# Softmax attention with PSUM banks picked by age instead of by name, and with new orders for its pairs of units

## Chip, cores and metric

One core of one Trainium2 chip runs the whole program. The metric is device time in microseconds (us), the median of several runs. A profile of one execution gives each engine's instructions: PE (TensorE matmuls), PEld (its weight loads), DVE (VectorE), ACT (ScalarE), POOL (GpSimd) and SP (SyncE, which issues DMAs).

## What is computed

A transformer block of 2048 tokens, 512 channels, in fp32: attention with 32 heads of 16 channels behind a layer norm, then a gated MLP whose gate mixes tokens. The change lies in the attention.

```python
def _A_ref(x, wqkv, wo):
    B, S, D = x.shape
    H = 32; Dh = D // H
    ...
    scale = Dh ** -0.5
    scores = jnp.einsum("bhqd,bhkd->bhqk", q, k) * scale
    p = _softmax(scores, axis=-1)
    o = jnp.einsum("bhqk,bhkd->bhqd", p, v)
    ...
h = x + _A_ref(_layernorm(x, axis=-1), A_wqkv, A_wo)
h2 = h + _B_ref(_layernorm(h, axis=-1), B_w_in, B_w_sp, B_b_sp, B_w_out)
```

## The kernel before

The program has three stages: projections (to about 165 us), the attention (to about 1350 us), and the rest. In the attention, heads go in eight groups of four (`hg`), queries in four blocks of 512 (`qb`), keys in sixteen blocks of 128 (`kb`). A **unit** is one `(hg, qb, kb)`: four score products of 128 keys by 512 queries, one for each head, four exponentials on ACT into one `pt` tile, and four products of `pt` with the values, which add up in one PSUM bank, `pv` (`weigh`, L718). A **block** is the sixteen units of one `(hg, qb)`; at its end ACT copies `pv` out (`gather`, L736).

The softmax needs the maximum of each row first. So eight more products for two units compute scores for a later block (`max_pair`, L218): four of kind M and two of kind m, each reduced by DVE (L241), and v and u, where ACT takes an absolute value (L246) and DVE combines it (L250). M uses the array's rows from 64 on, m, v and u those from 0 on. Of the score products, Sa uses the rows from 0 on and Sb those from 64 on. Two products that stand next to each other on different rows run side by side.

Every product, S or M, m, v, u, takes one of **seven PSUM banks**: m0 to m2 are numbers 0 to 2 (`ps_m`), s0 to s3 are numbers 3 to 6 (`ps_s`). The eighth is `pv`. A bank is free again when ACT or DVE has read it; PE waits for that at the product's weight load.

The order of the work is written out in lists that `play` (L751) goes through, for PE, ACT and DVE alike. In `"Sa5 M6 m3"` the letter is the kind of product and the number is the bank. `h` weighs half of the oldest finished unit (256 queries), `V` the whole of it. `N` reduces finished maxima on DVE, `T` transposes them and sends them off by DMA (or inverts sums), `G` is `gather`. `ORDER` (L42) is played for a pair of units (16 products), `FIRST_TWO` (L46) for a block's first two pairs (32 products), `START` (L45) once, for the very first pair. A list is cut into **groups** of products by its weighings: in `ORDER` six products, h, four, h, six, V. There are 245 such pairs: START 1, FIRST_TWO 30 times two, ORDER 184. The last eleven pairs are scheduled by other code, which the change leaves alone.

An ACT or DVE instruction that needs two semaphores gets an extra instruction ahead of it, which waits for the one (here PE's), while the instruction itself waits for the other. The first exponential of a unit is such a case, since its `pt` tile is new.

Of the kernel before, what the change touches and what calls it, by code (L numbers as in the profile page):

```python
# [34 lines left out]
MB = 3  # L35
# [3 lines left out]

ORDER = "Sa5 M6 m3 M2 v4 Sb1 h Sb6 u0 M5 Sa4 h Sb2 m3 Sb6 Sa1 N M4 Sa0 V T".split()  # L42

FOUR = "S S S S V S S S S H H H H S S S S V S S S S V V".split()
START = "Sa5 M6 m3 M2 v4 Sb1 f Sb6 u0 M5 Sa4 Sb2 m3 Sb6 Sa1 M4 Sa0 V".split()  # L45
FIRST_TWO = ("M5 Sa3 M2 Sa4 Sb1 Sb0 m6 h Sa4 M2 v3 m5 Sb1 M6 h u2 G Sa5 Sb3 m0 Sb4 M1 Sa6 V "  # L46
             "v0 M2 Sa3 M5 u1 Sb4 h h Sa2 Sb5 m6 M3 Sb1 Sa0 V").split()
RG = 64
VW = DH + 1
NF = 5  # L50
# [9 lines left out]
def block_kernel(ctx: ExitStack, tc: tile.TileContext, x, wqkv, wo, w_in, w_sp4, b_sp, w_out, out):  # L60
# [152 lines left out]
    def bank(i):  # L213
        if i in more:
            return more[i]()
        return ps_m.tile([P, 512], F32, name=f"m{i}")
# [59 lines left out]
    def max_rows():  # L276

        g, parts = turned.pop(0)
        t = sm.tile([P, 32], F32, name="mturned")
        nc.vector.transpose(t, parts.bitcast(F32).rearrange("p t j i -> p (t j i)"))  # L280
        for n in range(P // 32):
            for j in range(2):
                r0 = RG * j + KS
                nc.sync.dma_start(
                    qst[g][r0:r0 + 2].bitcast(F32).rearrange("r p (c n s) -> r (p c) n s", n=4, s=32)[:, :, n],
                    t[32 * n + 16 * j:32 * n + 16 * j + 16, :])


    with ExitStack() as pre:
# [178 lines left out]
        todo, done = [], [0]  # L468
# [203 lines left out]
    def invert():  # L672

        hg, cols, sums, pool = sums_.pop(0)
        rc = pool.tile([P, 16], F32, name="rcp")
        nc.vector.reciprocal(rc, sums)
        for j in range(4):
            nc.sync.dma_start(r_scr[head(hg, j % 2, j // 2), cols].rearrange("(p c) -> p c", c=16),
                              rc[32 * j:32 * j + 32, :])
# [3 lines left out]
    with ExitStack() as at:  # L683
# [10 lines left out]
        def new_pt():  # L694
            return pp.tile([P, 4, 512], F32, name="pt")

        def product(out, hg, qb, kb, t, p):

            r = slice(RG * t, RG * t + KM)
            nc.tensor.matmul(out, kst[hg % 2][r, p, kb * P:(kb + 1) * P], qst[hg * NQ + qb][r, p, :],  # L700
                             start=True, stop=True)

        def exp(out, scores):
            nc.scalar.activation(out, scores, AF.Exp, scale=DH ** -0.5)  # L704
# [13 lines left out]
        def weigh(unit, pt, places, cols=slice(0, 512)):  # L718

            hg, qb, kb = unit  # L720
            if kb == 0 and cols.start == 0:
                pv[0] = ps_v.tile([P, 512], F32, name="pv")
            for t, p in sorted(places, key=places.get):
                j = 2 * t + p
                c = (4 * kb + j) * VW
                nc.tensor.matmul(pv[0][32 * j:32 * j + 32, cols], vst[hg % 2][:, c:c + 32],  # L726
                                 pt[:, places[t, p], cols], start=kb == 0,
                                 stop=kb == NB - 1 and cols.stop == 512)
# [3 lines left out]
        def gather(hg, qb, pool=sm):  # L732

            o = pp.tile([P, 512], F32, name="o", bufs=1)
            if pool is sm and not later:
                nc.scalar.activation(o, pv[0], AF.Copy)  # L736
            else:
                nc.vector.tensor_copy(o[:, :256], pv[0][:, :256])
                if later and pool is sm:
                    nc.vector.tensor_copy(o[:, 256:], pv[0][:, 256:])  # L740
                else:
                    nc.scalar.activation(o[:, 256:], pv[0][:, 256:], AF.Copy)
            cols = slice(qb * 512, (qb + 1) * 512)
            sums = pool.tile([P, 16], F32, name="sums")
            for j in range(4):
                h = head(hg, j % 2, j // 2)
                nc.sync.dma_start(o_scr[h * DH:(h + 1) * DH, cols], o[32 * j:32 * j + DH, :])
                nc.sync.dma_start(sums[32 * j:32 * j + 32, :], o[32 * j + DH:32 * j + VW, :])
            sums_[0] = (hg, cols, sums, pool)

        def play(order, units):  # L751

            ending = pending[:]
            pending[:] = ends
            ends.clear()
            units = list(units)
            open_ = []
            for x in order:  # L760
                if x[0] == "S":
                    if not open_:
                        open_.extend([units.pop(0), new_pt(), {}])
                    unit, pt, places = open_
                    t = "ab".index(x[1])
                    p = sum(u == t for u, _ in places)
                    out = bank(int(x[2:]))
                    product(out, *unit, t, p)
                    exp(pt[:, len(places), :], out)
                    places[t, p] = len(places)  # L770
                    if len(places) == 4:
                        waiting.append([tuple(open_), 0])
                        open_.clear()
                elif x == "h":
                    h = waiting[0][1]
                    weigh(*waiting[0][0], slice(256 * h, 256 * h + 256))
                    waiting[0][1] += 1
                    if h:
                        done[0] = waiting.pop(0)[0][0]
                elif x == "V":  # L780
                    done[0] = waiting[0][0][0]
                    weigh(*waiting.pop(0)[0])
                elif x == "G":
                    gather(*done[0][:2])
                elif x == "f":

                    pv[0] = ps_v.tile([P, 512], F32, name="pv")
                    for j in range(4):
                        nc.tensor.matmul(pv[0][32 * j:32 * j + 32, :], vst[0][:, :32],
                                         vst[0][:, :512], start=True, stop=True)  # L790
                elif x == "N":
                    if ending:
                        ending.pop()()
                elif x == "T":
                    if turned:
                        max_rows()
                    elif done[0] is not None and done[0][2] == 5 and sums_:
                        invert()
                else:
                    steps_of[x[0]].pop(0)(int(x[1:]))  # L800
            assert not ending and not open_ and not units

        waiting, done, doubles = [], [None], []

        def play_four(units):

# [24 lines left out]
        steps_of = {kind: [] for kind in "Mmvu"}  # L831
# [43 lines left out]
        with tc.manual_schedule(engines={E.PE, E.Activation, E.DVE, E.SP}):  # L875
            for n in range(0, len(units), 2):
# [9 lines left out]
                steps, place = n // 2 + LEAD < 8 * HG * NQ, n % NB // 2  # L886
# [10 lines left out]
                if steps:  # L897
                    if place or not n:
                        if place != 1 or n == 2:
                            play(ORDER if n else START, units[n:n + 2])  # L900
                    else:
                        play(FIRST_TWO, units[n:n + 4])
                elif n % 4 == 0:
                    if n == 504:
                        load_o(h_rows[3])
                    play_four(units[n:n + 4])
                elif n < 492:
                    if pending:
                        pending.pop()()
                    for i in range(2):  # L910
                        pt = new_pt()
                        for p in range(2):
                            for step in score(units[n + i], p, pt):
                                step()
                        if i:
                            more_h(4)
                        weigh(*waiting.pop(0)[0])
                        waiting.append([(units[n + i], pt, PLACES), 0])
                    if turned:
                        max_rows()  # L920
# [17 lines left out]
    def quarter(pool, name, tag):  # L938
        return pool.tile([P, HB, PITCH], F32R, name=name, tag=tag)[:, :, :FC]

    T = {n: [quarter(zc, n, f"{n}_{i}") for i in range(2)]
         for n in ("t3", "t2", "n4", "t1")}
# [175 lines left out]
    with ExitStack() as fin:  # L1118
# [36 lines left out]
        f = [Slot(fs, f"f{i}") for i in range(3)]  # L1155
# [148 lines left out]
        def fetch_h(p):  # L1304
            h = [f2.tile([P, D], F32, name=f"h{i}", bufs=2 - i) for i in range(2)]
            for i in (1, 0):
                nc.sync.dma_start(h[i], h_scr[rows(p, i), :])
            return h
# [46 lines left out]
        for p in range(HB):  # L1355
            (q, _, z1), last = nxt, p + 1 == HB
            nxt = None if last else fetch(p + 1)
            h = fetch_h(p)
# [96 lines left out]
```

## Time and profile before

| what | value |
|---|---|
| three runs | 1821.95, 1823.29, 1823.30 us, median 1823.29 |
| the profiled execution | 1821.23 us, span 1819.4 us |
| PE, DVE, ACT busy over the span | 1811.2, 1505.7, 1380.1 us |
| PE, DVE, ACT busy in 600 to 700 us | 100.0, 93.0, 96.9 us |
| granted TensorE clock | 1.00 |

A row of the timeline has start, duration, engine, line, operation, output<-input and a count; what stands in brackets is the idle time ahead of it and what ended it. In the timeline tiles are named without their numbers: `s<-kst,qst` of L236 is a product for the maxima in one of the banks s0 to s3, `m<-qst,kst` of L700 is a score product in one of m0 to m2.

### The profile page before, as it was taken

What the parts mean: (1) busy time and instruction counts of PE and PEld (TensorE: products, weight loads), DVE (VectorE), ACT (ScalarE), POOL (GpSimd) and SP (SyncE); (2) the same over time, 40 slices, a digit from 0 to 9 for tenths busy, and PEclk for the clock granted to TensorE, in tenths of its full rate; (3) what the DMA queues carried; (4) which work ended last, traced back from release to release, by engine and by line L of the source; (5) the groups of instructions that cost most, each with busy time, mean ns of one, the idle gap of its engine ahead of it and who ended that gap; (6) DMA issues with size and microseconds to landing.
All of it is one profiled execution on the core that took longest, in us unless ns stands there. A gap on an engine that the chain in (4) does not pass through costs nothing.

```text
span 1819.4 us, 36269 instructions
## 1 busy us (share of the span) xinstructions
PE 1811.2 (100%) x13362; PEld 1040.9 (57%) x13362; DVE 1505.7 (83%) x3030; ACT 1380.1 (76%) x2676; POOL 226.0 (12%) x305
## 2 busy tenths in 40 slices
PE   9999999999999999999999999999999999999999
PEld 6875444444444444444444444444438889999998
DVE  6587999999999999999999999999926677877664
ACT  3224999999999999999999999999994444434221
POOL 2241000011010100000000000000110755001111
PEclk9999999999999999999999999999999999999999
DMA  6788111221120211022012011100215554768562
GB/s 197 196 194 204 42 25 31 48 56 29 40 58 17 55 41 25 20 48 39 14 40 43 19 38 40 26 14 17 40 51 138 168 171 162 229 193 279 188 197 90
DMA packets 148761, 160.17 MB, mean 88 GB/s; under 512 B 63096, under 2 KB 93320, under 8 KB 147240
## 3 DMA queue, kind: packets, MB, share of 16 engines
q1 hardware_dynamic: 143800, 146.44, 30.3%
q10 hardware_dynamic: 4752, 11.41, 1.6%
q8 instruction: 105, 1.72, 0.4%
q14 instruction: 72, 0.59, 0.1%
q0 software_dynamic: 32, 0.01, 0.0%
HBM read 101.26 MB, written 55.61 MB: 86 GB/s over the span
## 4 chain that ended last, share of the span: by engine, by line
PE 99%; DVE 1%; ACT 0%; issue 0%; DMA 0%; SPq 0%; DVEq 0%; ACTq 0%
PE pv L726 30%; PE s L700 15%; PE m L700 9%; PE s L236 8%; PE acc L107 6%; PE acc L109 6%; PE acc L108 5%; PE m L236 4%; PE g L109 4%; PE g L108 4%; PE g L107 4%; PE acc L645 2%; PE tp L1323 1%; PE acc L1344 0%; PE tp L1019 0%; PE tp L390 0%
## 5 line engine op out<-in xcount | busy, mean ns | idle before, releaser
L241 DVE TENSOR_REDUCE mx<-s 128x1 f32<-128x512 f32 x1135 | 727.7, 684 | 79.4 <-PE s L236 53.7
L704 ACT ACTIVATE pt<-s 128x512 f32<-128x512 f32 (+1 forms) x1084 | 650.6, 666 | 3.1 <-PE s L700 1.6
L726 PE MATMUL pv<-pt,vst 128*32 128x256 f32 (+1 forms) x6048 | 590.9, 466 | 0.0
L704 ACT ACTIVATE pt<-m 128x512 f32<-128x512 f32 x920 | 536.8, 618 | 37.6 <-PE s L236 26.2
L236 PE MATMUL s<-kst,qst 48*128 48x512 f32 x1135 | 445.2, 433 | 0.0
L700 PE MATMUL s<-qst,kst 50*128 50x512 f32 x1128 | 432.6, 456 | 0.5 <-ACT pt L704 0.5
L700 PEld LDWEIGHTS s<-qst,kst 50*128 50x128 f32 x1128 | 190.2, 184 | 266.6 <-DVE mx L241 179.7
L700 PE MATMUL m<-qst,kst 50*128 50x512 f32 x920 | 320.0, 432 | 0.0
L241 DVE TENSOR_REDUCE mx<-m 128x1 f32<-128x512 f32 x373 | 250.9, 684 | 11.5 <-PE m L236 10.9
L726 PEld LDWEIGHTS pv<-pt,vst 128*32 128x32 f32 x6048 | 123.6, 108 | 213.5 <-issue 202.0
L236 PEld LDWEIGHTS s<-kst,qst 48*128 48x128 f32 x1135 | 189.8, 185 | 58.8 <-ACT pt L704 27.5
L700 PEld LDWEIGHTS m<-qst,kst 50*128 50x128 f32 x920 | 150.7, 184 | 105.8 <-DVE mx L241 87.3
L250 DVE CUSTOM_DVE_ANT_0 ab<-m,ab 128x512 f32<-128x512 f32 x249 | 169.6, 681 | 0.6 <-PE m L236 0.5
L236 PE MATMUL m<-kst,qst 48*128 48x512 f32 x373 | 144.2, 416 | 0.0
L236 PE MATMUL m<-uvs,qst 48*128 48x512 f32 x282 | 137.1, 486 | 0.0
L246 ACT ACTIVATE ab<-s 128x512 f32<-128x512 f32 x215 | 136.8, 636 | 0.0
L101 POOL CAST mparts<-nm 128x16 fp32r<-128x16 f32 x32 | 6.3, 196 | 883.0 <-DVE nm L254 883.0
L236 PE MATMUL s<-uvs,qst 48*128 48x512 f32 x215 | 84.2, 392 | 0.0
L959 ACT ACTIVATE ws<-a 128x512 fp32r<-128x512 f32 x80 | 45.8, 621 | 48.7 <-PE g L109 23.8
L1038 ACT ACTIVATE z<-acc 128x464 f32<-128x464 f32 (+2 forms) x64 | 27.6, 457 | 67.3 <-PE acc L109 67.3
L236 PEld LDWEIGHTS m<-uvs,qst 48*128 48x128 f32 x282 | 51.6, 183 | 39.8 <-DVE mx L241 37.5
L107 PE MATMUL acc<-wi,hT 128*128 128x464 f32 (+2 forms) x196 | 72.8, 371 | 0.0
(210 smaller groups left out, 2592.7 us busy)
## 6 DMA issues: line engine op xcount, KB each, us to landing
a<-in_w_sp SPq DMA_DIRECT2D x80, 256.0 KB
qst<-q_scr SPq DMA_DIRECT2D x192, 64.0 KB
z_scr<-z ACTq DMA_DIRECT2D x32, 344.0 KB
kst<-k_scr SPq DMA_DIRECT2D x42, 256.0 KB
k_scr<-part SPq DMA_DIRECT2D x16, 512.0 KB
q_scr<-part SPq DMA_DIRECT2D x16, 512.0 KB
z<-z_scr SPq DMA_DIRECT2D x14, 344.0 KB
b<-z_scr SPq DMA_DIRECT2D x24, 172.0 KB
```

What stands on the lines that cost most here:

```text
L107: nc.tensor.matmul(ps, lh, rh, start=first, stop=False)
L108: nc.tensor.matmul(ps, lh, rl, start=False, stop=False)
L109: nc.tensor.matmul(ps, ll, rh, start=False, stop=last)
L236: nc.tensor.matmul(acc, q[r, p, c], keys[r, p], start=True, stop=True)
L241: nc.vector.reduce_max(at(t, e if t else e - 1), acc, axis=AX.X)
L246: nc.scalar.activation(ab[0], acc, AF.Abs)
L250: nc.vector.tensor_tensor_reduce(ab[0], acc, ab[0], 0.5, LOW, ALU.add, ALU.max, at(0, 0))
L645: yield nc.tensor.matmul(acc, o2[b][:, d, :], wo2[a][:, d, :], start=i == 0, stop=i == 3 * DB - 1)
L700: nc.tensor.matmul(out, kst[hg % 2][r, p, kb * P:(kb + 1) * P], qst[hg * NQ + qb][r, p, :], start=True, stop=True)
L704: nc.scalar.activation(out, scores, AF.Exp, scale=DH ** -0.5)
L726: nc.tensor.matmul(pv[0][32 * j:32 * j + 32, cols], vst[hg % 2][:, c:c + 32], pt[:, places[t, p], cols], start=kb == 0, stop=kb == NB - 1 ...
L959: nc.scalar.activation(hi, src, AF.Copy)
```

## The change

The number behind a letter is no longer a bank but a place in a list of the seven banks by age. `by_age` takes the bank at that place out of the list (0 is the one whose last use began longest ago), and puts it at the end. All three orders are new. `N` and `T` stand earlier in `ORDER`. The number of products of each kind, of weighings and of units is the same in each list. `ORDER` still has groups of six, four and six. `FIRST_TWO` had groups of seven, six, seven, six and six products, with two halves side by side in `h h`; it now has six, four, six, six, four and six.

```diff
-ORDER = "Sa5 M6 m3 M2 v4 Sb1 h Sb6 u0 M5 Sa4 h Sb2 m3 Sb6 Sa1 N M4 Sa0 V T".split()
+ORDER = "Sa0 M0 Sa2 M0 m1 Sb0 h Sb0 Sa0 M0 N m0 h v0 Sb1 Sa0 M0 u1 T Sb0 V".split()
...
-FIRST_TWO = ("M5 Sa3 M2 Sa4 Sb1 Sb0 m6 h Sa4 M2 v3 m5 Sb1 M6 h u2 G Sa5 Sb3 m0 Sb4 M1 Sa6 V "
-             "v0 M2 Sa3 M5 u1 Sb4 h h Sa2 Sb5 m6 M3 Sb1 Sa0 V").split()
+FIRST_TWO = ("Sb0 m0 M2 Sa0 M1 Sa0 h v0 Sb0 M0 u1 h G Sa0 M1 Sb0 Sa0 m1 Sb0 V Sb0 m0 Sa0 M0 Sa1 "
+             "M0 h Sb0 Sa1 M0 m0 h v0 M0 Sa0 Sb0 u1 Sb0 V").split()
...
+        def by_age(place):
+
+            ages.append(ages.pop(int(place)))
+            return ages[-1]
...
-                    out = bank(int(x[2:]))
+                    out = bank(by_age(x[2:]))
...
-                    steps_of[x[0]].pop(0)(int(x[1:]))
+                    steps_of[x[0]].pop(0)(by_age(x[1:]))
...
-        waiting, done, doubles = [], [None], []
+        waiting, done, doubles, ages = [], [None], [], list(range(MB + 4))
```

ACT in the middle of the attention, from the first product of a pair's third group on. Tiles are named with their numbers: `m2_14028` is bank m2, the number behind counts tiles. Before, the first row waits for PE and for a second semaphore, and the absolute value (`ab`) comes sixth:

```order
L704 ACTIVATE pt_14027<-m2_14028 128x512 [waits PE_49,Activation_49]
L704 ACTIVATE pt_14027<-s3_14034 128x512 [waits PE_49]
L704 ACTIVATE pt_14027<-m1_14037 128x512 [waits PE_49]
L704 ACTIVATE pt_14027<-m0_14043 128x512 [waits PE_49]
L704 ACTIVATE pt_14050<-s2_14051 128x512 [waits PE_49,Activation_49]
L246 ACTIVATE ab_14065<-s1_14063 128x512 [waits PE_49]
L704 ACTIVATE pt_14050<-m1_14067 128x512 [waits PE_49]
```

The same place of ACT in the changed program (its lines are one lower):

```order
L245 ACTIVATE ab_14029<-s3_14027 128x512 [waits PE_49]
L703 ACTIVATE pt_14013<-s0_14031 128x512 [waits PE_49]
L703 ACTIVATE pt_14013<-m2_14034 128x512 [waits PE_49]
L703 ACTIVATE pt_14013<-s1_14043 128x512 [waits PE_49]
L703 ACTIVATE pt_14050<-m1_14051 128x512 [waits PE_49,Activation_49]
L703 ACTIVATE pt_14050<-s2_14057 128x512 [waits PE_49]
L703 ACTIVATE pt_14050<-m2_14066 128x512 [waits PE_49]
```

The absolute value has moved from the sixth place to the first, and what comes first now waits for PE alone.

PE, the second group of the next pair, up to the first product of its third group, before. The last of the four products, in bank s1, waits for ACT:

```order
L700 MATMUL s3_14074<-qst_12329,kst1_1733 128x512 [waits DVE_49]
L236 MATMUL m0_14077<-uvs1_1734,qst_12877 128x512
L236 MATMUL s2_14080<-kst1_1733,qst_12877 128x512 [waits Activation_49]
L700 MATMUL s1_14083<-qst_12329,kst1_1733 128x512 [waits Activation_49]
L726 MATMUL pv_13925<-pt_14027,vst1_104 32x256 x4
L700 MATMUL m2_14091<-qst_12329,kst1_1733 128x512 [waits DVE_49]
```

The same place of PE in the changed program:

```order
L699 MATMUL s1_14073<-qst_12329,kst1_1733 128x512
L699 MATMUL m1_14077<-qst_12329,kst1_1733 128x512 [waits Activation_49]
L235 MATMUL s3_14080<-kst1_1733,qst_12877 128x512 [waits DVE_49]
L235 MATMUL s2_14083<-kst1_1733,qst_12877 128x512 [waits Activation_49]
L725 MATMUL pv_13912<-pt_14013,vst1_104 32x256 x4
L235 MATMUL s0_14090<-uvs1_1734,qst_12877 128x512 [waits DVE_49]
```

The last product of this group was Sa in s1, and is m in s2; it waits in both for the sixth row of ACT above (s1_14063 before, s2_14057 now). The first product of the third group was Sb and is v.

PE in `FIRST_TWO`, around its fourth weighing, before: both halves stand side by side (x8 is two times four products).

```order
L236 MATMUL s2_2380<-kst0_105,qst_1334 128x512
L236 MATMUL m1_2383<-uvs0_106,qst_1334 128x512 [waits DVE_49]
L700 MATMUL s1_2386<-qst_1185,kst0_105 128x512 [waits Activation_49]
L726 MATMUL pv_2365<-pt_2308,vst0_103 32x256 x8
L700 MATMUL m2_2398<-qst_1185,kst0_105 128x512 [waits DVE_49]
```

The same place of PE in the changed program:

```order
L699 MATMUL m0_10082<-qst_8483,kst1_1733 128x512 [waits DVE_49]
L235 MATMUL s3_10085<-kst0_105,qst_9035 128x512 [waits Activation_49]
L725 MATMUL pv_10064<-pt_10045,vst1_104 32x256 x3
L725 MATMUL pv_10064<-pt_10045,vst1_104 32x256 [waits Activation_49]
L699 MATMUL s2_10092<-qst_8483,kst1_1733 128x512
L699 MATMUL s0_10096<-qst_8483,kst1_1733 128x512 [waits DVE_49]
L235 MATMUL m2_10099<-kst0_105,qst_9035 128x512 [waits Activation_49]
L235 MATMUL m1_10102<-kst0_105,qst_9035 128x512 [waits Activation_49]
L725 MATMUL pv_10064<-pt_10045,vst1_104 32x256 x4
```

The halves are now apart, with a group of four products between them, so PE changes from products to weighing six times in a block's first two pairs where it did so five times.

More of the change, by code (lines that the diff above doesn't have):

```diff
@@ L37 @@
 FIRST = 1
-ORDER = "Sa5 M6 m3 M2 v4 Sb1 h Sb6 u0 M5 Sa4 h Sb2 m3 Sb6 Sa1 N M4 Sa0 V T".split()
+ORDER = "Sa0 M0 Sa2 M0 m1 Sb0 h Sb0 Sa0 M0 N m0 h v0 Sb1 Sa0 M0 u1 T Sb0 V".split()
 FOUR = "S S S S V S S S S H H H H S S S S V S S S S V V".split()
-START = "Sa5 M6 m3 M2 v4 Sb1 f Sb6 u0 M5 Sa4 Sb2 m3 Sb6 Sa1 M4 Sa0 V".split()
-FIRST_TWO = ("M5 Sa3 M2 Sa4 Sb1 Sb0 m6 h Sa4 M2 v3 m5 Sb1 M6 h u2 G Sa5 Sb3 m0 Sb4 M1 Sa6 V "
-             "v0 M2 Sa3 M5 u1 Sb4 h h Sa2 Sb5 m6 M3 Sb1 Sa0 V").split()
+START = "Sa0 M0 Sa2 M0 m1 Sb0 f Sb0 Sa0 M0 m0 v0 Sb1 Sa0 M0 u1 Sb0 V".split()
+FIRST_TWO = ("Sb0 m0 M2 Sa0 M1 Sa0 h v0 Sb0 M0 u1 h G Sa0 M1 Sb0 Sa0 m1 Sb0 V Sb0 m0 Sa0 M0 Sa1 "
+             "M0 h Sb0 Sa1 M0 m0 h v0 M0 Sa0 Sb0 u1 Sb0 V").split()
 RG = 64
```

## The prediction, on record before the run

> **What bounds the kernel now.** I read the page first: which engine is busy, and what the chain that ended last is made of.
>
> ```profile
> PE 1811.2 (100%) x13362; PEld 1040.9 (57%) x13362; DVE 1505.7 (83%) x3030; ACT 1380.1 (76%) x2676; POOL 226.0 (12%) x305
> ...
> PE 99%; DVE 1%; ACT 0%; issue 0%; DMA 0%; SPq 0%; DVEq 0%; ACTq 0%
> ```
>
> PE looks like the only bound, and DMA and SP's queue release nothing. But the change works in the attention alone, so next I took busy time by stretch, and the copies that end its blocks.
>
> ```profile
> 600.00:700.00 100.00, 100.00 (x848) 42.28 (x844) 93.00 (x180) 96.86 (x195) 2.88 (x11) 1.00 0.19 38
> ```
>
> ```profile
> L736 ACT ACTIVATE o<-pv x30: 675/692/701, 207.4 to 1302.9; 128x512 f32<-128x512 f32 x30
> ```
>
> PE, ACT and DVE (the first, fourth and third share) are all nearly full, and 29 blocks of eight pairs take 1302.9 - 207.4 = 1095.5 us, 37.78 each. With three engines this close, a share decides nothing; I follow one ordinary pair, from the timeline.
>
> ```profile
> 603.33 0.49 PE L700 MATMUL m<-qst,kst 50*128 50x512 f32 x1
> ...
> 603.33 0.50 PE L236 MATMUL s<-kst,qst 48*128 48x512 f32 x1
> ...
> 603.91 0.60 ACT L704 ACTIVATE pt<-m 128x512 f32<-128x512 f32 x1 [0.17 <-PE s L236]
> ...
> 604.23 1.07 PE L726 MATMUL pv<-pt,vst 128*32 128x512 f32 x8
> 604.41 0.59 ACT L704 ACTIVATE pt<-s 128x512 f32<-128x512 f32 x1
> 604.89 1.09 ACT L704 ACTIVATE pt<-m 128x512 f32<-128x512 f32 x2
> ...
> 605.23 0.50 PE L700 MATMUL s<-qst,kst 50*128 50x512 f32 x1
> ...
> 605.58 0.40 PE L236 MATMUL m<-kst,qst 48*128 48x512 f32 x1
> ...
> 605.79 1.29 DVE L241 TENSOR_REDUCE mx<-s 128x1 f32<-128x512 f32 x2 [0.39 <-PE s L236]
> ...
> 605.81 0.39 PE L700 MATMUL m<-qst,kst 50*128 50x512 f32 x1
> 605.84 0.63 ACT L704 ACTIVATE pt<-s 128x512 f32<-128x512 f32 x1
> ...
> 606.13 0.64 PE L726 MATMUL pv<-pt,vst 128*32 128x256 f32 x8
> 606.32 0.64 ACT L246 ACTIVATE ab<-s 128x512 f32<-128x512 f32 x1
> 606.70 0.50 PE L700 MATMUL s<-qst,kst 50*128 50x512 f32 x1
> ...
> 607.01 0.18 PEld L700 LDWEIGHTS s<-qst,kst 50*128 50x128 f32 x1
> ...
> 607.04 0.47 PE L700 MATMUL s<-qst,kst 50*128 50x512 f32 x1
> ...
> 607.44 0.64 PE L726 MATMUL pv<-pt,vst 128*32 128x256 f32 x8
> ...
> 608.01 0.49 PE L700 MATMUL m<-qst,kst 50*128 50x512 f32 x1
> ```
>
> ACT is idle once in the pair: at 603.91 it waits for the third group's first product, although PE began that at 603.33. PE waits once too: the weight load at 607.01 (Sa4, the second group's last) comes just after the `ab` that ends at 606.32 + 0.64 = 606.96 and frees its bank; its product takes 0.47 where the one beside it on time took 0.39. The two waits make one **loop**:
>
> - third group starts 603.33, its first product ends 0.49 later, ACT starts 0.09 after that;
> - that exponential takes 0.60, to 604.51; five more ACT instructions end at 606.96, 2.45 us later, 0.49 each;
> - 0.05 to the weight load, 0.43 from there to the weighing at 607.44, 0.57 to the next third group at 608.01.
>
> The sum is 0.49 + 0.09 + 0.60 + 2.45 + 0.05 + 0.43 + 0.57 = 4.68, and 608.01 - 603.33 is 4.68. So an ordinary pair takes what this loop takes. PE without the stall: groups of six take 606.13 - 605.23 = 0.90 (a slot of two products 0.23, from 605.58 to 605.81), one of four 0.67, a half 0.57, the whole 1.00; in all 2 x 0.90 + 0.67 + 2 x 0.57 + 1.00 = 4.61. ACT's nine instructions need 9 x 0.49 = 4.41. DVE is idle 0.39 ahead of 605.79. A new order can therefore win at most 0.07 in an ordinary pair, and can lose much more.
>
> **The ordinary pair after.** The number of products, weighings and groups is the same, so PE's 4.61 and ACT's 4.41 stay. What can change is the loop. I followed the new list's places to banks (the rows of ACT and PE in the section on the change): the second group's last product, m, gets the bank of Sa2 from the group before. ACT's order from the third group is v, Sb, Sa, Sb, Sa, Sa2: Sa2 is the sixth instruction, as `ab` was. **The loop has the same links and the same five steps of 0.49.** One link differs. Its first ACT instruction was the first exponential of a unit, which waits for PE through an extra instruction; now it is v's absolute value, which waits for PE itself. Two rows of the projections, of equal shape, show what that is worth:
>
> ```profile
> 161.62 0.39 PE L109 MATMUL acc<-xT,wqk 128*128 128x512 f32 x1
> ...
> 162.05 0.60 ACT L99 ACTIVATE part<-acc 128x512 fp32r<-128x512 f32 x1 [2.95 <-PE acc L109]
> ...
> 164.36 0.39 PE L109 MATMUL acc<-xT,wqk 128*128 128x512 f32 x1
> ...
> 164.84 0.60 ACT L99 ACTIVATE part<-acc 128x512 fp32r<-128x512 f32 x1 [2.19 <-PE acc L109]
> ```
>
> The one at 162.05 holds the wait for PE itself and starts 0.04 after the product's end. At 164.84 the wait stands in the extra instruction, and it is 0.09, as at 603.91. No row of the attention shows ACT idle ahead of a direct wait; the nearest there is DVE's at 605.79, 0.06 after the product that began at 605.23 ended. So the link saves 0.03 to 0.05; I take 0.05, as ACT's own rows have it, which gives 4.63, still above PE's 4.61. Mid-way the extra instruction costs nothing: 605.84 has one ahead of it, and its end, 606.47, is 0.49 after the one before it.
>
> 184 pairs play `ORDER`; 30 of them follow `FIRST_TWO` and are counted with it. 154 x 0.05 = **7.7 us**.
>
> **A block's first two pairs.** Here the trace has
>
> ```profile
> 619.29 0.50 PE L236 MATMUL s<-kst,qst 48*128 48x512 f32 x1
> ...
> 626.01 1.07 PE L726 MATMUL pv<-pt,vst 128*32 128x256 f32 x16
> ...
> 627.01 0.50 PE L700 MATMUL m<-qst,kst 50*128 50x512 f32 x1
> ...
> 627.60 0.60 ACT L704 ACTIVATE pt<-m 128x512 f32<-128x512 f32 x1 [0.21 <-PE s L700]
> ...
> 629.05 0.49 PE L700 MATMUL s<-qst,kst 50*128 50x512 f32 x1
> ...
> 633.64 0.50 PE L700 MATMUL s<-qst,kst 50*128 50x512 f32 x1
> ```
>
> 9.76 for the two pairs and 4.59 for the ordinary one behind, 14.35 in all. ACT's 16 exponentials, two absolute values and the copy need 19 x 0.49 = 9.31; 0.45 is lost, part of it at 627.60. In the old list same-row products stand together (Sb1 Sb0; v3 m5), so its 32 products need 18 slots of two where 16 would do. The new list always alternates: 16 slots. Against that it changes to weighing six times, not five. One change costs 0.90 - 3 x 0.23 = 0.21 in a group and 0.57 - 0.43 = 0.14 at a half (side by side two halves take 1.00, so 0.43 more than one), together 0.35; two slots save 0.46. PE gains 0.1.
>
> Going through the list with these durations, ACT still has 0.2 us of work when the second group's first product is ready, 0.3 to 0.4 at the third to fifth, and runs dry only at the sixth, whose first product is v again. There it loses what an ordinary pair loses: 4.63 - 4.41 = 0.22. That gives 9.31 + 0.22 = 9.53, and 4.63 behind it: 14.16, a gain of 0.19; 30 x 0.19 = **5.7 us**. Bounds for the two pairs alone: 9.31 if ACT never runs dry, 9.76 + 0.35 = 10.11 if the sixth change comes on top of the old time. I take the value between, since all but the first of those ACT margins are as large as a whole change.
>
> **Other edits.**
>
> ```profile
> 600.62 0.24 DVE L676 RECIPROCAL rcp<-sums 128x16 f32<-128x16 f32 x1
> ...
> 609.41 0.21 DVE L254 TENSOR_REDUCE nm<-mx 128x16 f32<-128x64 f32 x1
> ...
> 610.21 0.21 DVE L280 STREAM_TRANSPOSE mturned<-mparts 128x32 f32<-128x32 f32 x1
> ```
>
> ```profile
> 166.59 0.64 PE L789 MATMUL pv<-vst 128*32 128x512 f32 x4 [0.94 <-DVE part L104]
> ```
>
> `N` and `T` move these three on DVE, each once a block and never two of them by more than 0.42 in one pair, about DVE's idle 0.39; without that cover they cost 30 x 0.66 = 20 us. Their DMAs go on SP's queue up to a weighing earlier; PE's chain has no DMA in it. `START` is played once; in it PE waits 0.94 for banks before and may wait as much more or less now, so within 1 us, taken as nothing.
>
> Sum: 7.7 + 5.7 = 13.4. The profiled execution took 1821.2 (span 1819.4 and 1.8 around it) and becomes 1807.8. The median, 1823.3, lies 2.1 above it; I forecast **1810** for the median.
>
> **The rivals.**
> *The loop doesn't shorten.* The latency in the attention is the same for a direct wait; only `FIRST_TWO` gains: 9.31 + 0.27 + 4.68 = 14.26, 30 x 0.09 = 2.7, so 1820.6. For it: no row shows that link there. Against: 0.09 at 603.91 is the very number of the extra instruction's row.
> *Half of it.* 0.03 for the link, as DVE's row has it: 154 x 0.03 + 30 x 0.15 = 9.1, so 1814.
> *One more change of mode decides.* If ACT's 0.2 at `FIRST_TWO`'s second group is not there, PE and ACT fall into step group by group, each of six changes is paid in the open, and the two pairs take 10.11: 30 x 0.35 = 10.5 lost. With an unchanged loop that is 1834; with the loop shortened it turns the sum from 7.7 / 30 = 0.26 lost at each `FIRST_TWO`. Against: in the old list ACT lost 0.45 with only five. The Trainium skill, TensorEngine Tiling (Array Packing), Key Properties, speaks for it: changing the tiling mode drains TensorE. The trace agrees, with the 0.35 above; by that rule alone, 24 changes a block instead of 23, the sum would be 10.5 us slower.
> *More than forecast.* The loop falls to PE's 4.61, and ACT never runs dry in `FIRST_TWO`: 154 x 0.07 + 30 x 0.43 = 24 less, 1799.
>
> **How the numbers follow.** Forecast 0.55, half of it 0.13, unchanged loop 0.15, slower 0.10, more 0.07. 0.2% is 3.6 us, about what a measurement of this kernel can tell from no change: faster means below 1819.7, slower above 1826.9. Faster 0.55 + 0.13 + 0.07 = 0.75; same 0.15; slower 0.10. The range, 1802 to 1822, has the first three and a part of the last.
>
> **What would show it.** In the changed profile, gathers 37.3 apart instead of 37.78. In an ordinary pair, the ACT row with idle time ahead is `ab`, 0.04 after its product, and third groups are 4.63 apart. In `FIRST_TWO`, ACT is idle once, and its two pairs take 9.5. It is wrong if idle time of ACT shows at other rows, if `ab` starts 0.09 after its product, or if first slots of groups wait for DVE.

## The result, and the profile after

The changed kernel takes **1808.49 us** (median of four runs, 1808.48 to 1809.07); the kernel before took 1822.76 beside it (four runs, 1821.95 to 1823.30). The ratio is 0.9923, with a 95% interval from 0.9906 to 0.9940: 14.3 us less, with 11 to 17 as its bounds. In later comparisons the kernel before took 1821.68 to 1822.22, which would make it 13.2 to 13.7. The profiled execution took 1808.49, with a span of 1806.7 at a granted clock of 1.00.

Busy shares and the chain say as little as before. On the page of the changed kernel:

```profile
PE 1797.7 (99%) x13362; PEld 1047.6 (58%) x13362; DVE 1496.7 (83%) x3030; ACT 1380.2 (76%) x2676; POOL 226.4 (13%) x305
...
PE 99%; DVE 1%; issue 0%; ACT 0%; DVEq 0%
```

In the stretch from 600 to 700 us, the first share is PE's, the third DVE's, the fourth ACT's:

```profile
600.00:700.00 100.00, 99.91 (x860) 43.23 (x858) 92.77 (x181) 97.99 (x197) 2.44 (x10) 1.00 0.19 40
```

ACT was busy for 96.86% of this stretch and is for 97.99%: the same instructions in less time. The copies that end the blocks, with the first and last start behind the durations:

```profile
L735 ACT ACTIVATE o<-pv x30: 642/645/658, 206.3 to 1288.7; 128x512 f32<-128x512 f32 x30
```

29 blocks take 1288.7 - 206.3 = 1082.4 us, 37.32 each; before they took 1095.5. That is 13.1 us less, and the whole span is 12.7 less (1819.4 - 1806.7): the ends of the program give 0.4 back. (The copy itself stands 1.0 us earlier in `FIRST_TWO` than it did, which shifts both its first and its last start.)

One ordinary pair of the changed kernel, from its timeline:

```profile
602.20 1.11 ACT L703 ACTIVATE pt<-m 128x512 f32<-128x512 f32 x2
...
602.89 0.49 PE L235 MATMUL s<-uvs,qst 48*128 48x512 f32 x1
...
603.41 0.60 ACT L245 ACTIVATE ab<-s 128x512 f32<-128x512 f32 x1
...
603.91 1.08 ACT L703 ACTIVATE pt<-s 128x512 f32<-128x512 f32 x2
...
605.87 0.59 ACT L703 ACTIVATE pt<-m 128x512 f32<-128x512 f32 x1
...
606.51 0.18 PEld L235 LDWEIGHTS m<-kst,qst 48*128 48x128 f32 x1
...
606.60 0.41 PE L235 MATMUL m<-kst,qst 48*128 48x512 f32 x1
...
606.93 0.64 PE L725 MATMUL pv<-pt,vst 128*32 128x256 f32 x8
...
607.50 0.50 PE L235 MATMUL s<-uvs,qst 48*128 48x512 f32 x1
```

v's product ends at 602.89 + 0.49 = 603.38 and `ab` starts at 603.41, 0.03 later, where the exponential in its place started 0.09 after its product. ACT's last instruction before ended at 602.20 + 1.11 = 603.31, so its idle time is 0.10 where it was 0.17. The second group's last product still waits for ACT: its weight load, at 606.51, comes 0.05 after the sixth instruction from `ab` on, which ends at 605.87 + 0.59 = 606.46. The product, at 606.60, takes 0.41; 0.39 is its time without a wait, and before the change it took 0.47. From third group to third group it is 607.50 - 602.89 = 4.61; the mean of all ordinary pairs is 4.63.

Grouped by who waited for whom between 300 and 1200 us (us in total, times, longest), most of ACT's waits in the loop of the kernel before are one row:

```profile
ACT pt L704 <- PE s L236: 20.2, 116, 0.2
```

The changed kernel has no row for `ab` there. That does not mean that the wait is gone: the view counts only waits above 0.15 us, and that of `ab` is 0.10. In this stretch of the whole trace ACT stands idle 169 times ahead of `ab`, which starts 0.033 after a product's end at the median; in the kernel before it stood idle 168 times ahead of an exponential, which started 0.093 after. The loop is still there, with a shorter wait.

And `FIRST_TWO` of the changed kernel, from its first product to the one of the pair behind, and on to the next pair:

```profile
614.02 0.49 PE L699 MATMUL m<-qst,kst 50*128 50x512 f32 x1
...
621.33 0.75 ACT L703 ACTIVATE pt<-s 128x512 f32<-128x512 f32 x1
...
621.66 0.50 PE L235 MATMUL s<-uvs,qst 48*128 48x512 f32 x1
...
622.20 0.60 ACT L245 ACTIVATE ab<-s 128x512 f32<-128x512 f32 x1
...
623.56 0.49 PE L699 MATMUL s<-qst,kst 50*128 50x512 f32 x1
...
628.18 0.50 PE L699 MATMUL m<-qst,kst 50*128 50x512 f32 x1
```

9.54 for the two pairs and 4.62 behind them. ACT is idle once, ahead of the sixth group's `ab`: from 621.33 + 0.75 = 622.08 to 622.20. That `ab` ends at 622.80, 0.72 after 622.08 where a step takes 0.49, so 0.23 is lost there.

### The profile page after: what moved, and what is told of

Read it like the earlier page. It is cut to its first block, busy times and chain, and to the rows that moved or that the text cites. A ratio compares the mean times of both kernels' runs of the same rounds, so it can differ in the third digit from the quotient of the medians.

```text
span 1806.7 us, 36120 instructions
## 1 busy us (share of the span) xinstructions
PE 1797.7 (99%) x13362; PEld 1047.6 (58%) x13362; DVE 1496.7 (83%) x3030; ACT 1380.2 (76%) x2676; POOL 226.4 (13%) x305
## 3 DMA queue, kind: packets, MB, share of 16 engines
q8 instruction: 105, 1.72, 0.4%
## 4 chain that ended last, share of the span: by engine, by line
PE 99%; DVE 1%; issue 0%; ACT 0%; DVEq 0%
PE pv L725 30%; PE s L699 12%; PE s L235 8%; PE m L235 8%; PE m L699 7%; PE acc L106 6%; PE acc L108 6%; PE acc L107 6%; PE g L108 4%; PE g L107 4%; PE g L106 4%; PE acc L644 2%; PE tp L1327 1%; PE acc L1348 0%; PE tp L1023 0%; PE tp L389 0%
## 5 line engine op out<-in xcount | busy, mean ns | idle before, releaser
L240 DVE TENSOR_REDUCE mx<-s 128x1 f32<-128x512 f32 x856 | 555.9, 683 | 46.0 <-PE s L235 40.0
L703 ACT ACTIVATE pt<-m 128x512 f32<-128x512 f32 x815 | 475.1, 620 | 0.0
L240 DVE TENSOR_REDUCE mx<-m 128x1 f32<-128x512 f32 x652 | 430.3, 683 | 39.7 <-PE m L235 35.0
L235 PE MATMUL s<-kst,qst 48*128 48x512 f32 x856 | 313.2, 421 | 0.0
L699 PEld LDWEIGHTS s<-qst,kst 50*128 50x128 f32 x1233 | 189.3, 184 | 207.4 <-DVE mx L240 128.1
L235 PE MATMUL m<-kst,qst 48*128 48x512 f32 x652 | 242.7, 420 | 0.0
L235 PEld LDWEIGHTS s<-kst,qst 48*128 48x128 f32 x856 | 151.5, 185 | 8.3 <-ACT pt L703 0.4
L235 PEld LDWEIGHTS m<-kst,qst 48*128 48x128 f32 x652 | 114.2, 185 | 13.3 <-issue 2.8
L249 DVE CUSTOM_DVE_ANT_0 ab<-m,ab 128x512 f32<-128x512 f32 x147 | 100.1, 681 | 0.2 <-issue 0.2
L245 ACT ACTIVATE ab<-s 128x512 f32<-128x512 f32 x142 | 85.3, 601 | 13.8
L235 PEld LDWEIGHTS s<-uvs,qst 48*128 48x128 f32 x244 | 44.6, 183 | 66.4 <-DVE mx L240 44.5
```

The costliest lines, as they stand in the source:

```text
L235: nc.tensor.matmul(acc, q[r, p, c], keys[r, p], start=True, stop=True)
L240: nc.vector.reduce_max(at(t, e if t else e - 1), acc, axis=AX.X)
L245: nc.scalar.activation(ab[0], acc, AF.Abs)
L249: nc.vector.tensor_tensor_reduce(ab[0], acc, ab[0], 0.5, LOW, ALU.add, ALU.max, at(0, 0))
```

## The experiments

Nine kernels ran. Below, "a block" is the last start of the copy `o<-pv` less the first, by 29; "the two pairs" and "an ordinary pair" are times from a list's first product to the next list's, each the median over the blocks of the whole trace. By the same count the kernel before has 9.72 for the two pairs, 4.61 for the pair behind and 4.68 to 4.70 for the rest, and the changed kernel 9.53, 4.63 and 4.63. Each ratio is taken against runs of the kernel before made beside that kernel (medians of 1821.68 to 1822.76); the row "before" has those beside the changed one.

| kernel | median us | ratio to before, 95% interval | a block | the two pairs | an ordinary pair |
|---|---|---|---|---|---|
| before | 1822.76 | 1 | 37.78 | 9.72 | 4.68 |
| changed | 1808.49 | 0.9923 (0.9906 to 0.9940) | 37.32 | 9.53 | 4.63 |
| two bank numbers exchanged in the old `ORDER` | 1812.87 | 0.9952 (0.9939 to 0.9964) | 37.49 | 9.72 | 4.63 |
| one change of mode fewer | 1815.90 | 0.9969 (0.9958 to 0.9981) | 37.58 | 9.78 | 4.63 |
| m in the bank of ACT's next instruction | 1898.63 | 1.0420 (1.0404 to 1.0436) | 40.27 | 9.54 | 5.12 |
| m in a bank of DVE | 1840.40 | 1.0103 (1.0089 to 1.0117) | 38.37 | 9.53 | 4.81 |
| new `FIRST_TWO` alone | 1830.45 | 1.0049 (1.0036 to 1.0062) | 38.06 | 9.99 | 4.69 |
| new `ORDER` alone | 1824.33 | 1.0014 (1.0005 to 1.0023) | 37.86 | 9.80 | 4.63 |
| half of the absolute value | 1801.72 | 0.9890 (0.9875 to 0.9905) | 37.11 | 9.35 | 4.63 |
| the copy on DVE | 1821.42 | 0.9996 (0.9987 to 1.0005) | 37.76 | 9.94 | 4.63 |
| the copy on DVE, `FIRST_TWO` arranged for it | 1809.40 | 0.9930 (0.9918 to 0.9942) | 37.36 | 9.61 | 4.63 |

**Two bank numbers exchanged.** The kernel before, with nothing of the change:

```diff
-ORDER = "Sa5 M6 m3 M2 v4 Sb1 h Sb6 u0 M5 Sa4 h Sb2 m3 Sb6 Sa1 N M4 Sa0 V T".split()
+ORDER = "Sa5 M6 m3 M2 v4 Sb1 h Sb6 u0 M5 Sa4 h Sb6 m3 Sb2 Sa1 N M4 Sa0 V T".split()
```

> The kernel before with two bank numbers exchanged in ORDER and nothing else: the third group now takes Sb6 m3 Sb2 instead of Sb2 m3 Sb6. Bank 2 was last read by DVE, bank 6 by ACT, so the third group's first product already waits for ACT, and its exponential needs to wait for PE alone. Theory (the loop of 4.68 us starts with an instruction that waits through an extra one): ACT starts 0.03 to 0.04 after that product instead of 0.09, the pair takes 4.63, 154 x 0.05 to 0.06 = 8 to 9 us less, a median of 1814 to 1815, and no row of ACT has the extra instruction with idle time ahead. Rival (the gain comes from the new arrangement, the banks by age or v's place in it): no change, 1822.8 within 1 us. Second rival (the extra instruction only moves to the product Sb2 that now waits for DVE in the middle, and costs its 0.05 there): no change either, but with the short start of 0.04 in the third group.

It took 1812.87, 8.8 us less than the 1821.68 of the kernel before beside it. What line 704 issued in the kernel before:

```profile
L704 ACTq EVENT_SEMAPHORE  x448: 17/17/651, 173.9 to 1363.6; - x150
```

With the two numbers exchanged:

```profile
L704 ACTq EVENT_SEMAPHORE  x264: 17/17/656, 176.2 to 1355.3; - x132
```

448 - 264 = 184 extra instructions are gone, one for each play of `ORDER`, and third group follows third group at 4.63:

```profile
600.23 0.49 PE L700 MATMUL s<-qst,kst 50*128 50x512 f32 x1
...
604.86 0.50 PE L700 MATMUL s<-qst,kst 50*128 50x512 f32 x1
```

```profile
L736 ACT ACTIVATE o<-pv x30: 670/672/675, 207.5 to 1294.7; 128x512 f32<-128x512 f32 x30
```

The blocks lose (1302.9 - 207.4) - (1294.7 - 207.5) = 8.3 us, while the two pairs at a block's start keep their 9.72. So the link is worth 0.057 in each of the five undisturbed ordinary pairs (8.3 / 29 / 5), and neither v's place nor banks by age are needed for it. Two numbers in the old list do it. Both rivals fall.

It also corrects the reason given ahead of the prediction. The third group's first product still belongs to a new unit with a new `pt` tile, and its exponential needs no extra instruction all the same. What decides here is who read the product's bank last. The likely reason, read from the lists and not tested by itself, is that with a bank that ACT read the product itself has waited for ACT.

**One change of mode fewer.** The changed kernel, with the first two groups of `FIRST_TWO` in one:

```diff
-FIRST_TWO = ("Sb0 m0 M2 Sa0 M1 Sa0 h v0 Sb0 M0 u1 h G Sa0 M1 Sb0 Sa0 m1 Sb0 V Sb0 m0 Sa0 M0 Sa1 "
+FIRST_TWO = ("Sb0 m0 M2 Sa0 M1 Sa0 v0 Sb0 M0 u1 V G Sa0 M1 Sb0 Sa0 m1 Sb0 V Sb0 m0 Sa0 M0 Sa1 "
```

> The changed kernel with its FIRST_TWO alone edited: the groups M1 Sa0 h v0 Sb0 M0 u1 h G become M1 Sa0 v0 Sb0 M0 u1 V G, so that ten products stand in a row and one weighing of a whole unit follows; five weighings instead of six in a block's first two pairs, 30 changes of mode fewer in the program. Theory (the loop through ACT and the banks sets the time, not the changes): no gain; ten products need more banks than seven, so the last ones wait for ACT, the two pairs take 9.54 to 9.8 us, and the median is 1808 to 1816. Rival (each change of mode is paid in the open, 0.35 us): 30 x 0.35 = 10.5 us less, 1798.

7.4 us slower than the changed kernel, at the slow end of what the banks gave. Its timeline, the ten products in a row:

```profile
616.58 0.50 PE L699 MATMUL m<-qst,kst 50*128 50x512 f32 x1
...
617.39 0.43 PE L235 MATMUL m<-uvs,qst 48*128 48x512 f32 x1
617.83 0.50 PE L699 MATMUL m<-qst,kst 50*128 50x512 f32 x1
...
618.32 0.50 PE L235 MATMUL m<-uvs,qst 48*128 48x512 f32 x1
...
618.75 1.07 PE L725 MATMUL pv<-pt,vst 128*32 128x512 f32 x8
```

With slots of 0.23 the ten would be on their way by 616.58 + 0.11 + 4 x 0.23 = 617.61 (the 0.11 is by how much a group's first product is longer); the last starts at 618.32. These 0.7 of waiting for banks outweigh the 0.35 saved; with what later groups wait less, the two pairs take 9.78 instead of 9.53, 0.25 x 30 = 7.5. So the run refutes the rival's 1798, but it adds a wait while it takes out a change, and does not price the change alone.

**m in the bank of ACT's next instruction.** The changed kernel, with one place changed:

```diff
-ORDER = "Sa0 M0 Sa2 M0 m1 Sb0 h Sb0 Sa0 M0 N m0 h v0 Sb1 Sa0 M0 u1 T Sb0 V".split()
+ORDER = "Sa0 M0 Sa2 M0 m1 Sb0 h Sb0 Sa0 M0 N m3 h v0 Sb1 Sa0 M0 u1 T Sb0 V".split()
```

> The changed kernel with one place in ORDER changed: the second group's last product is m3 instead of m0, so that it takes the bank whose reader is ACT's next instruction, one later in ACT's order, and the loop has six steps of ACT instead of five. Theory (the loop sets the pair): 4.62 + 0.49 = 5.11 us, 184 x 0.49 = 90 us more, a median of about 1898, ACT idle ahead of v's absolute value as before and PE waiting about half a us ahead of that product. Rival (PE, 99.9% busy, sets the pair, and a wait of half a us at one weight load is hidden by queues): under 20 us more, below 1828.

1898.63, against 1898 expected. In its timeline:

```profile
603.81 0.50 PE L235 MATMUL s<-uvs,qst 48*128 48x512 f32 x1
...
606.79 1.08 ACT L703 ACTIVATE pt<-s 128x512 f32<-128x512 f32 x2
...
607.50 0.93 PE L235 MATMUL s<-kst,qst 48*128 48x512 f32 x2
...
607.93 0.18 PEld L235 LDWEIGHTS s<-kst,qst 48*128 48x128 f32 x1 [0.47 <-ACT pt L703]
...
608.93 0.50 PE L235 MATMUL s<-uvs,qst 48*128 48x512 f32 x1
...
609.46 0.60 ACT L245 ACTIVATE ab<-s 128x512 f32<-128x512 f32 x1 [0.60 <-PE m L699]
```

The two products from 607.50, on different rows, take 0.93 where side by side they take 0.39: the second's weight load comes at 607.93, 0.06 after ACT's sixth step behind `ab` ended at 606.79 + 1.08 = 607.87. The pair is 608.93 - 603.81 = 5.12, one step of 0.49 more than 4.63, and ACT is idle 0.60 ahead of `ab` instead of 0.10. The loop sets the pair. PE's share in the stretch from 600 to 700 us hardly shows it:

```profile
600.00:700.00 100.00, 99.55 (x804) 39.51 (x800) 87.89 (x168) 91.20 (x184) 5.40 (x8) 1.00 0.16 38
```

PE is still 99.55% busy, with half a us of waiting in each pair; the counts and the shares of ACT and DVE, both lower, are what shows that the work got slower.

**m in a bank of DVE.** The same place, with `m1` for `m0`:

```diff
+ORDER = "Sa0 M0 Sa2 M0 m1 Sb0 h Sb0 Sa0 M0 N m1 h v0 Sb1 Sa0 M0 u1 T Sb0 V".split()
```

> The changed kernel with one place in ORDER changed: the second group's last product is m1 instead of m0, so that it takes a bank that DVE's reduction of an M frees instead of ACT's sixth instruction. Theory: the loop through ACT is gone, but that reduction ends later than ACT's sixth instruction, as DVE works through four reductions of 0.65 us and two combinations first; a loop through DVE takes its place, about 0.15 to 0.2 us longer than 4.62, 184 x 0.165 = 30 us more, about 1838. Rival (the loop through ACT is the only thing above PE's 4.61): the pair falls to 4.61 or stays at 4.62, 1806 to 1808.5.

1840.40, and 4.81 a pair:

```profile
604.95 1.28 DVE L240 TENSOR_REDUCE mx<-s 128x1 f32<-128x512 f32 x2
...
605.58 0.39 PE L235 MATMUL m<-kst,qst 48*128 48x512 f32 x1
605.68 0.50 PE L235 MATMUL s<-kst,qst 48*128 48x512 f32 x1
```

The first of DVE's two reductions ends near 605.63, and m starts at 605.68, 0.10 behind its partner, takes 0.11 longer than its 0.39, and holds up the weighing by 0.2. There is no free bank in these lists: to leave ACT's loop is to enter DVE's.

**Each list alone.** First the new `FIRST_TWO` with the old `ORDER` and `START`, then the new `ORDER` and `START` with the old `FIRST_TWO`. A small addition to `by_age` takes "=5" as the name of a bank, so that old lists keep their numbers:

```diff
-            ages.append(ages.pop(int(place)))
+            if place[0] == "=":
+                ages.remove(int(place[1:]))
+                ages.append(int(place[1:]))
+            else:
+                ages.append(ages.pop(int(place)))
             return ages[-1]
```

> The changed kernel's FIRST_TWO, its banks by age, with ORDER and START of the kernel before, whose banks keep their numbers. If the two gains add (ordinary pairs 0.058 us each, as exchanging two bank numbers of the kernel before showed; a block's first two pairs and the pair behind them 0.168), this one has the second alone: 30 x 0.168 = 5 us less than before, about 1817. Theory of the banks: FIRST_TWO hands on seven banks in the order of its own last uses, and the old list, played by name, takes them in another one; the first ordinary pair behind then waits for banks, about 0.25 us, and the two pairs themselves take 9.6, so that a block takes 37.9 instead of 37.78: about 5 us slower than before, 1826.

> The changed kernel's ORDER and START, its banks by age, with FIRST_TWO of the kernel before, whose banks keep their numbers. If the gains add: the ordinary pairs' alone, 5 a block of 0.058 us, 30 x 0.29 = 8.7 us less than before, about 1813. Theory of the banks: ordinary pairs take 4.63, but the old FIRST_TWO meets banks that are released in another order than its numbers, and takes 9.95 instead of 9.73; a block is 37.73 against 37.78, about 1820 to 1821.

Neither is faster than before: 1830.45 and 1824.33, 8.8 and 2.6 us slower than the 1821.69 beside them. Neither gain comes by itself. Both lose at the seam, though where I had put it only in part. The new `FIRST_TWO` alone:

```profile
622.19 0.50 PE L699 MATMUL s<-qst,kst 50*128 50x512 f32 x1
...
623.91 0.50 PE L235 MATMUL m<-uvs,qst 48*128 48x512 f32 x1
...
632.17 0.49 PE L699 MATMUL s<-qst,kst 50*128 50x512 f32 x1 [0.19 <-ACT pt L703]
```

Its first group takes 623.91 - 622.19 = 1.72 instead of 0.90 + 0.57 = 1.47, and the first product of the pair behind waits until ACT frees its bank; 9.98 in all. I had expected 9.6, and the wait within the pair behind. The old `FIRST_TWO` alone, where it begins:

```profile
618.84 1.06 PE L725 MATMUL pv<-pt,vst 128*32 128x512 f32 x8
...
620.13 0.50 PE L235 MATMUL s<-kst,qst 48*128 48x512 f32 x1 [0.22 <-DVE mx L249]
```

A group would follow this weighing 1.00 later, at 619.84; it starts at 620.13, since its bank is still with DVE. That makes the pair ahead of the list 4.91 instead of 4.63, and the two pairs 9.80. A list leaves seven banks behind in the order of its last uses, and the next one has to begin with those that come free first. So the seam does cost more than either list gains, but in both I was about 4 us too low on its price, and had the second just below the kernel before.

**Half of the absolute value.** The changed kernel, with v's absolute value and its combination over 256 of 512 columns, which leaves half of v's and u's columns out of the maximum:

```diff
-            ab[0] = sm.tile([P, 512], F32, name="ab")
-            nc.scalar.activation(ab[0], acc, AF.Abs)
+            ab[0] = sm.tile([P, 256], F32, name="ab")
+            nc.scalar.activation(ab[0], acc[:, :256], AF.Abs)
...
-            nc.vector.tensor_tensor_reduce(ab[0], acc, ab[0], 0.5, LOW, ALU.add, ALU.max, at(0, 0))
+            nc.vector.tensor_tensor_reduce(ab[0], acc[:, :256], ab[0], 0.5, LOW, ALU.add, ALU.max, at(0, 0))
```

> The changed kernel with v's absolute value taken over 256 of its 512 columns, and combined by DVE over these 256 (it leaves half of v's and u's columns out of the maximum). ACT's first instruction of the loop gets about 0.2 us shorter. Theory (behind the loop of 4.62 stands PE with 4.61): the loop would be 4.4, but PE's six groups allow no less than 4.60 to 4.61, so a pair gains 0.01 to 0.02 and the median is 1803 to 1807; ACT is idle about 0.2 us in each pair. Rival (PE is not near its limit, the loop alone sets the pair): 184 x 0.2 = 37 us less, about 1772.

1801.72. Its stretch from 600 to 700 us, and its copies:

```profile
600.00:700.00 100.00, 100.00 (x866) 42.71 (x860) 87.66 (x182) 96.04 (x198) 2.43 (x10) 1.00 0.21 43
```

```profile
L735 ACT ACTIVATE o<-pv x30: 597/599/602, 205.9 to 1282.2; 128x512 f32<-128x512 f32 x30
```

The rival falls: with 0.2 taken out of ACT's loop and DVE down from 92.77 to 87.66%, the ordinary pair only goes from 4.629 to 4.625. I had put the bound at PE's own 4.61, but the timeline does not show PE free of waits:

```profile
602.06 0.62 ACT L703 ACTIVATE pt<-m 128x512 f32<-128x512 f32 x1
...
602.78 0.60 ACT L703 ACTIVATE pt<-s 128x512 f32<-128x512 f32 x1
...
603.28 0.59 ACT L703 ACTIVATE pt<-m 128x512 f32<-128x512 f32 x1
...
603.92 0.18 PEld L235 LDWEIGHTS m<-kst,qst 48*128 48x128 f32 x1
```

ACT now stands idle a second time in the pair, from 602.68 to 602.78, ahead of the first group's first exponential; and the weight load of the second group's last product still comes 0.05 after an exponential, which ends at 603.28 + 0.59 = 603.87. So a second loop through ACT, from the first group on, stands where the first one stood. Whether PE's own time is 4.61 or nearer to 4.625 stays open.

What I had left out is that the two pairs of `FIRST_TWO` hold two absolute values as well: they go from 9.53 to 9.35, 0.18 x 30 = 5.4 of the 6.8 us. DVE's combinations became shorter too, so the run does not separate the two engines. But in these two pairs of the changed kernel ACT is idle for 0.11 us and DVE for 0.74 (medians over the blocks), so ACT's work, as the prediction had it, is the likelier cause.

**The copy on DVE.** That pointed to taking the copy of `pv` off ACT at a block's end:

```diff
-                nc.scalar.activation(o, pv[0], AF.Copy)
+                nc.vector.tensor_copy(o, pv[0])
```

> The changed kernel with the copy of pv at a block's end on DVE instead of ACT; the lists stay. The kernel with half an absolute value showed that a block's first two pairs end on ACT (9.35 us with ACT relieved of 0.4 us, 9.53 without). Theory A (ACT alone sets those two pairs): ACT loses one step of 0.49, the two pairs take about 9.3, 30 x 0.2 = 6 us less than the changed kernel, 1802. Theory B (DVE is as near: 14 reductions and combinations of 0.6 us there, and the copy comes in the middle of them): the copy adds 0.6 to DVE in the two pairs, the banks behind it come free later, and PE waits 0.3 to 0.4 us more than now: 30 x 0.4 = 12 us more, 1820.

1821.42, 12.9 us slower than the changed kernel. Theory B's size was right, its place was not:

```profile
621.98 0.68 DVE L735 COPY o<-pv 128x512 f32<-128x512 f32 x1
...
622.81 1.07 PE L725 MATMUL pv<-pt,vst 128*32 128x512 f32 x8 [0.71 <-DVE o L735]
```

The copy comes late in DVE's queue, and what waits for it is the next weighing, which needs `pv`, and not a product that needs a bank. The two pairs take 9.94, 0.41 more, times 30 is 12.5.

The other kernel has the copy on DVE and a `FIRST_TWO` with few reductions ahead of it, in five weighings:

```diff
+FIRST_TWO = ("Sa0 M3 m3 Sb1 M0 Sa1 Sb0 V Sb0 G m0 m0 Sa0 M0 Sa1 Sb0 V Sa0 M1 Sb0 m2 M0 Sb0 "
+             "Sa0 h M0 Sa0 v0 M0 h Sb0 u1 M1 v1 Sa0 u0 Sb0 h h").split()
```

> The copy on DVE as before, with a FIRST_TWO arranged for it: V and V in place of the first four halves' pairs, the reductions ahead of the copy few, v and u both in the second pair. Five weighings follow one another with one change of mode fewer than the changed kernel's six. Theory: ACT has 18 steps of 0.49 = 8.8 in the two pairs and the copy meets DVE when it has little behind it, so PE sets them: 9.35 to 9.45 instead of 9.53, 30 x 0.1 = 3 us less, about 1805. Rival (DVE's copy delays the banks again): 1808 to 1815.

1809.40, level with the changed kernel within what can be told (their ratios' intervals overlap):

```profile
L735 DVE COPY o<-pv x30: 690/692/692, 206.1 to 1289.6; 128x512 f32<-128x512 f32 x30
```

(1289.6 - 206.1) / 29 = 37.36 a block, and 9.61 for the two pairs, where I had expected 9.35 to 9.45. The time fell into the rival's 1808 to 1815. Its groups of seven leave a product without a partner, which costs PE a slot of 0.23 each. Still, an estimate from the prediction's durations gives PE's own work in this list as 4 x 1.13 + 0.67 + 2 x 0.57 + 3 x 1.00 = 9.33, so most of the miss is waiting: the first group takes 2.35 to the next, the second, also seven products and a whole weighing, 2.13. Which bank the first group waits for was not separated. No kernel that computes the whole reference beat the changed one.

## Why the prediction was right

The forecast was 1810 for the median, and it came to 1808.49. By its steps:

- **The ordinary pair is a loop through ACT and a bank.** Shown: moving the loop's end by one ACT instruction costs one step of 0.49 in every pair, as reckoned, though PE is over 99% busy in either. In the changed kernel the same loop still sets the pair, or stands within 0.02 of what does.
- **The link is worth 0.05, 154 times, 7.7 us.** The mechanism is shown by the two exchanged numbers alone. The size was a little low: 0.09 to 0.03, not to 0.04, 0.057 in a pair by the blocks, 8.3 us between the first and the last copy (and those hold 145 such pairs, not 154). The rivals "doesn't shorten" and "half of it" are out.
- **`FIRST_TWO` and the pair behind gain 0.19, 5.7 us.** The two pairs take 9.53, as worked out from 19 steps of ACT and one loss of 0.22, and ACT is idle where it was said to be, with 0.23 lost. They took 9.72 before and not the 9.76 of the one place read, and the pair behind 4.61 and not 4.59; so the gain is (9.72 + 4.61) - (9.53 + 4.63) = 0.17, 5.0 us. The term that was mis-sized is the old time, read at a single block. Which of the edits to `FIRST_TWO` gives the gain (fewer slots, the halves apart, the order of the banks) no run separated.
- **PE's 4.61 stands close behind.** With ACT relieved the pair stays at 4.625, where a second loop through ACT remains; so 4.61 is neither shown nor refuted, and another order with these groups could win at most the 0.02 down to it.
- **One more change of mode decides.** It doesn't: that rival had the two pairs at 10.11, and they take 9.53. The Trainium skill, TensorEngine Tiling (Array Packing), Key Properties, says that changing the tiling mode drains TensorE. The kernel before agrees in that a change costs PE time, 0.35 by the prediction's rows. An estimate from the same rows gives PE's own work in the new list, all six changes in it, as 4 x 0.90 + 2 x 0.67 + 4 x 0.57 + 2 x 1.00 = 9.22, less than the 9.53 that ACT needs; so the sixth change would be hidden. That is argued from durations, and no run adds or takes out a change without other waits.
- **Where the wait for PE stands.** That a direct wait starts sooner was taken from two rows of the projections and holds in the attention. The Trainium skill, Perfetto Trace Analysis, Identifying Dependency Chains, says that an instruction which waits for several engines may get such an extra instruction ahead of it. The traces agree, and add its price when the engine is idle: 0.06.
- **`N`, `T` and `START` at nothing.** 0.4 us at the program's ends is all that the span shows beside the blocks; which edit it belongs to was not separated. `START` waits 0.94 ahead of its first product on `pv` in both kernels.

The closeness of the sum is in part luck: between the copies the link gave 0.6 more than forecast and `FIRST_TWO` 0.7 less. And what I had not weighed is the seam. I treated the pairs and `FIRST_TWO` as two gains to be added. They do add, 8.3 and 5.0 against the 13.1 that the blocks show, but only since both lists came together: either alone made the kernel slower.

## What to carry to other kernels

When three engines are all over 90% busy, follow one period in the timeline and close the loop: which wait ends last, and how many instructions lie between a buffer's reader and the product that takes it next. A wait for two semaphores costs its extra instruction only where the engine stands idle, so let the instruction that an idle engine starts with wait for one, by choosing which engine read its buffer last. And an order by hand must be judged with its neighbours: the order in which one list frees the buffers is the next list's start.

## What the runs showed of the hardware

The extra instruction, 17 ns long at the median of line 704, delays an idle ACT by 0.06 us (0.093 against 0.033 from the product's end, medians of 168 and 169 waits), and nothing in the row read where ACT still had work (605.84 in the prediction). Whether it is there at all depends in this program on the engine that last read the product's PSUM bank, which an exchange of two numbers turned round 184 times. The busy share of PE is no measure of its waits: 99.91% in the changed kernel, 100.00% before and with half an absolute value, and 99.55% where half a us of waiting was added to each pair of 5.12.
